# Order and pace of the weight loads between the two halves of a transformer layer

## The chip, the cores and the metric

The kernel runs on one core of one Trainium2 chip. The metric is the device time of one execution in microseconds (us); the program before the change took 205.26 us, the median of three runs (205.18, 205.26 and 205.62).

## What is computed

One layer on 2048 rows of width 448 in bf16: a linear attention with a learned feature map, then a gated feed-forward part, each behind a layernorm and with a residual. Cut to what matters:

```python
def _A_ref(x, wqkv, w_phi, wo):            # 16 heads of 28
    q, k, v = split_heads(x @ wqkv)
    pq, pk = q @ w_phi, k @ w_phi          # per head
    phi_q = concat([softmax(pq), softmax(-pq)]); phi_k = likewise of pk
    kv = einsum("bhsf,bhsd->bhfd", phi_k, v); z = phi_k.sum(s)
    o = (phi_q @ kv) / (phi_q @ z + 1e-6)
    return o @ wo
def _B_ref(x, w_gate, w_up, w_down):       # 448 -> 1792 -> 448
    return (sigmoid(x @ w_gate) * (x @ w_up)) @ w_down
h = x + _A_ref(layernorm(x), wqkv, w_phi, wo)
h2 = h + _B_ref(layernorm(h), w_gate, w_up, w_down)
```

## The kernel before, in words

The rows are cut into 16 tiles of 128. Three stretches follow one another. In the first, each tile is normed, transposed (xT4 to xT15 by DMA transposes that SP issues), multiplied by the folded key weights and by the value weights (pva, pvb), its features made (ek, ss, rs, phi) and its share added to the sum over all rows that the attention needs (the kv products kva0 to kva15 and kvb0 to kvb15, line 304 by way of `both`, in banks 6 and 7 of PSUM). In the transition, that sum is masked into kvz, the query features come from pqa and pqb with exponentials on ScalarE (eq, line 690), and per tile come num (the numerator and denominator), then on VectorE rsm, qq, b, c and rden (lines 767 to 775), the quotient o (line 779, on GpSimd or VectorE), its transpose oT (for tiles 0 and 1 on TensorE, line 506, for the others a DMA transpose that SP issues, line 792), the output projection woa and wob, a second layernorm and hT. In the third stretch, gate and up products ga and gb (line 304 by way of `pair`, line 876) alternate with the down products (dn, dp, later dm, line 908), each of which feeds an output store.

Nothing is planned at run time. The order of the instructions on each engine is written out by hand in `ORDER`, one list of names for each of SP, ScalarE (act), TensorE (pe), VectorE (dve) and GpSimd (pool). `Graph.op` records what each named operation reads and writes, and `Graph.emit` gives each one the semaphore waits that its dependencies (`deps`) call for; the engine works its list in order, so an instruction that waits holds all behind it on the same engine. SP's list holds all loads, transposes and stores. The weights of the transition and of the third stretch are 19 loads on SP's list (line 406), none of which waits for anything:

- ld_woe0, ld_woe1, ld_woo0, ld_woo1: the output projection, 336, 56, 336 and 56 KB, in rows of 896 bytes; first used by woa0 and wob0
- ld_wg0 to ld_wg3 and ld_wu0 to ld_wu3: gate and up, 448 KB each but 224 KB for ld_wg1 and ld_wu2, in rows of 3584 bytes. Every ga and gb depends on all eight of them (`wgu_keys`), so that ga0_1, the first, waits for the last to land
- ld_wd0 to ld_wd6: down, 224 KB each, in rows of 896 bytes; a down product over hidden columns ff needs ld_wd(ff // 2), and dn0_0 is the first

On SP's list before the change they stand behind the transpose xT15: sixteen of them in one row, in a mixed order, then oT2, then ld_wd0, ld_wu2 and ld_wd4, then oT3.

On TensorE's list the end of the first stretch reads "... pqa0_1 kvb12 pqb0_1 kva13 pqa1_0 kvb13 kva14 pqb1_0 kvb14 kva15 kvb15 qs pqa1_1 num0 pqb1_1 num1 pqa2_0 num2 pqb2_0 pqa2_1 oT0 oT1 pqb2_1 num3 woa0 wob0 num4 ... num6 ga0_1". One pq of the a kind is 8 matmuls, of the b kind 6; a kv product is 8, qs 32, a num 16. On VectorE's list: "kvzA kvzC kvzD rsm0 qq0 b0 c0 b1 rden0 c1 rsm2 rden1 qq2 b2 c2 rden2 o2 rsm3 qq3 b3 c3 rden3 bs2_0 ...". GpSimd makes o0, o1 and o3. num2 writes banks 6 and 7; pqa2_0 and pqb2_0 banks 0 and 1, pqa2_1 and pqb2_1 banks 4 and 5, which the exponentials eq1_1p and eq1_1m read before.

Of the kernel before, what the change touches and what calls it, by code (L numbers as in the profile page):

```python
# [18 lines left out]
class Graph:  # L19
# [86 lines left out]
    def emit(self, nc):  # L106
# [108 lines left out]
ORDER = {  # L215
# [6 lines left out]
    ),  # L222
# [60 lines left out]
    ),  # L283
}
PROGRAM = (
# [35 lines left out]
def build(nc, A_x, A_wqkv, A_w_phi, A_wo, B_w_gate, B_w_up, B_w_down, out):  # L321
# [10 lines left out]
    with ExitStack() as es:  # L332
# [66 lines left out]
        g = Graph()  # L399
# [163 lines left out]
        for kt in range(KT):  # L563
            b = (0, 1, 4, 5)[kt]
# [337 lines left out]
        def down1(t, b, parts, w=0):  # L902
            hb = hhT[(t // 4) % NHH]
            for nm, b, lo, hi in (("dm", b, 0, D - w), ("dl", 4, D - w, D))[:1 + (w > 0)]:
                for a, n in parts if nm == "dm" else ((0, 12), (12, 2)):
                    def f(e, a=a, n=n, b=b, lo=lo, hi=hi):
                        for ff in range(a, a + n):
                            p = e.matmul(bk(b)[:, lo:hi], lhsT=hb[:, ff, TS(t)], rhs=wd_sb[:, ff, lo:hi], start=ff == 0, stop=ff == FT - 1)  # L908
                        return p
                    op("pe", "%s%d_%d" % (nm, t, a), f,  # L910
                       r=[("hh", (t // 4) % NHH, ff, t % 4) for ff in range(a, a + n)] + [("wd", ff // 2) for ff in range(a, a + n)], w=[B(b)])
                finish(t, b, lo, hi, "" if nm == "dm" else "b")
# [9 lines left out]

        for step in PROGRAM.split():
            k, _, v = step.partition(":")
# [20 lines left out]
            elif k == "down1":  # L945
                down1(v[0], v[1], late, *v[2:])

        g.emit(nc)
        return g


def bass_sequential_preLN__linear_kernel_hedgehog__glu_gated_glu__prompt_kernel(
    nc, A_x, A_wqkv, A_w_phi, A_wo, B_x, B_w_gate, B_w_up, B_w_down, out
):
    build(nc, A_x, A_wqkv, A_w_phi, A_wo, B_w_gate, B_w_up, B_w_down, out)
# [28 lines left out]
```

## Time and profile before

| what | before |
|---|---|
| median of three runs | 205.26 us (205.18 to 205.62) |
| the profiled execution, its own time | 204.9 us |
| its span in the profile | 203.1 us |
| TensorE busy | 195.6 us, 96% of the span |
| VectorE, ScalarE, GpSimd busy | 134.7, 95.1 and 55.1 us |
| HBM read and written | 8.34 MB and 1.84 MB |

The profile is of one execution; times in it count from the start of the span, and what lies around the span (204.9 - 203.1 = 1.8 us) is not in it. PE is TensorE's matmuls, PEld its weight loads (one before each matmul), DVE is VectorE, ACT ScalarE, POOL GpSimd; SP only issues DMAs. A row of a timeline gives start, duration, engine, line, operation and tiles, and in square brackets how long the engine was idle before and what released it. The chain of waits is followed back from the last instruction and shown in order of time; "issue" in it is time in which the engine waited for nothing that the profile shows. A row of the windows view gives, for a stretch A:B, its length, then busy time and count of instructions of each engine, the granted clock, the mean busy share of the 16 DMA engines and what they moved in GB/s. A row of the DMA view gives a queue, its kind, packets, MB and share.

### The profile page before, as it was taken

The page shows a single profiled execution, that of the slowest core. Times are in us where ns is not written, and L with a number is a line of the kernel's source. Part 1 is how long each engine was busy: PE and PEld are TensorE (multiplying, and loading weights), DVE is VectorE, ACT ScalarE, POOL GpSimd, SP SyncE. Part 2 cuts the span into 40 slices and gives each one's busy share as a digit, 9 for nine tenths or more (in the row PEclk, how much of TensorE's full clock was granted, in tenths as well). Part 3 has the DMA queues.
Part 4 walks back from the last instruction along what each step waited for, and adds up shares of the span by engine and source line. Part 5 has one row for each costly group of instructions (what it writes and reads, how often), then busy time and mean ns, then how long its engine had stood idle before and what let it go on. Part 6 is the DMA issues. An engine that isn't in the chain of part 4 may idle for free.

```text
span 203.1 us, 5881 instructions
## 1 busy us (share of the span) xinstructions
PE 195.6 (96%) x2508; PEld 109.8 (54%) x2508; DVE 134.7 (66%) x328; ACT 95.1 (47%) x191; POOL 55.1 (27%) x97
## 2 busy tenths in 40 slices
PE   7899999997979999999999999999999999999995
PEld 2734555664448777777444544444555555554443
DVE  5899999977898897858667967526532422262224
ACT  3987989986982527222333343323422222222220
POOL 5698899613045303700023020001400000000000
PEclk9999999999999999999999999999999999999999
DMA  5966544999472411241004411030212000004003
GB/s 151 318 133 131 56 83 82 321 276 356 103 112 52 55 31 29 44 88 26 3 3 95 108 26 26 3 74 24 58 43 57 0 0 3 0 3 136 0 0 94
DMA packets 32867, 16.27 MB, mean 80 GB/s; under 512 B 25096, under 2 KB 31944, under 8 KB 32840
## 3 DMA queue, kind: packets, MB, share of 16 engines
q1 hardware_dynamic: 32336, 15.86, 32.9%
q8 instruction: 20, 0.33, 0.7%
q10 hardware_dynamic: 504, 0.03, 0.2%
q14 instruction: 7, 0.06, 0.1%
HBM read 8.34 MB, written 1.84 MB: 50 GB/s over the span
## 4 chain that ended last, share of the span: by engine, by line
PE 88%; DVE 6%; POOL 2%; issue 1%; DMA 1%; DVEq 0%
PE psum L304 81%; PE psum L908 5%; DVE st L513 2%; DMA x_sb<-in_A_x_dram 1%; DVE c_sb L773 1%; DVE b_sb L770 1%; POOL rst L526 1%; DVE st L798 1%; PE psum L581 0%; PE psum L506 0%; DVE mv L514 0%; POOL xn_pad L542 0%; DVE xnT L499 0%; POOL rst L816 0%; DVE rden L775 0%
## 5 line engine op out<-in xcount | busy, mean ns | idle before, releaser
L304 PE MATMUL psum<-xnT,wg_sb 64*128 64x512 bf16 (+1 forms) x490 | 93.1, 333 | 0.2 <-DVE rden L775 0.2
L304 PE MATMUL psum<-xnT,wu_sb 64*128 64x512 bf16 (+1 forms) x490 | 92.9, 333 | 0.0
L880 ACT ACTIVATE sg_sb<-psum 128x512 bf16<-128x512 f32 (+1 forms) x70 | 34.8, 511 | 91.5 <-PE psum L304 91.0
L881 DVE SCALAR_TENSOR_TENSOR hhT<-sg_sb,psum 128x512 bf16<-128x512 bf16 (+1 forms) x70 | 38.9, 576 | 53.2 <-ACT sg_sb L880 52.9
L304 PEld LDWEIGHTS psum<-xnT,wg_sb 64*128 64x128 bf16 x490 | 44.2, 94 | 23.3 <-DVE hhT L881 4.9
L304 PEld LDWEIGHTS psum<-xnT,wu_sb 64*128 64x128 bf16 x490 | 44.2, 94 | 13.4
L304 PE MATMUL psum<-wd_sb,hhT 64*128 64x448 bf16 x336 | 36.8, 349 | 0.0
L304 PEld LDWEIGHTS psum<-wd_sb,hhT 64*128 64x128 bf16 x336 | 17.0, 94 | 15.0 <-DVE x_sb L805 0.5
L304 PE MATMUL psum<-Wk,xnT 64*128 64x448 bf16 x112 | 22.0, 351 | 0.3 <-ACT Wk L499 0.2
L304 PE MATMUL psum<-wv_sb,xnT 64*128 64x448 bf16 x112 | 22.1, 351 | 0.1
L814 POOL TENSOR_SCALAR ve<-ssq 128x1 f32<-128x1 f32 x11 | 2.6, 234 | 57.8 <-ACT junk L811 57.5
L654 POOL TENSOR_TENSOR phi<-hhT,rs 128x896 bf16<-128x896 bf16 x10 | 16.9, 1701 | 2.5 <-DVE rs L650 1.6
L644 DVE TENSOR_REDUCE ss<-hhT 128x32 f32<-128x896 bf16 x16 | 16.9, 1063 | 0.5 <-ACT hhT L641 0.5
L690 ACT ACTIVATE eq<-psum 120x1024 bf16<-120x1024 f32 x16 | 15.7, 1026 | 2.7 <-PE psum L304 2.7
L304 PE MATMUL psum<-xnT,Wq 64*120 64x512 bf16 x112 | 14.7, 383 | 0.1
L304 PE MATMUL psum<-wo_o,oT 64*128 64x448 bf16 x56 | 13.2, 349 | 0.0
L304 PE MATMUL psum<-wo_e,oT 64*128 64x448 bf16 x56 | 13.1, 349 | 0.0
L915 DVE SCALAR_TENSOR_TENSOR x_sb<-psum,x_sb 128x448 bf16<-128x448 f32 (+2 forms) x17 | 9.4, 592 | 2.7 <-PE psum L908 1.6
L908 PE MATMUL psum<-wd_sb,hhT 128*128 128x448 bf16 (+2 forms) x70 | 11.1, 316 | 0.0
L304 PEld LDWEIGHTS psum<-Wk,xnT 64*128 64x128 bf16 x112 | 7.9, 94 | 5.9 <-PE psum L304 0.5
L779 POOL TENSOR_TENSOR o_pad<-c_sb,rden 128x448 bf16<-128x448 bf16 x8 | 7.4, 935 | 11.9 <-DVE rden L775 11.8
L770 DVE TENSOR_TENSOR b_sb<-psum,qq 128x464 bf16<-128x464 f32 x16 | 10.2, 638 | 0.3
(99 smaller groups left out, 236.4 us busy)
## 6 DMA issues: line engine op xcount, KB each, us to landing
out_dram<-x_sb SPq DMA_DIRECT2D x15, 112.0 KB, 1.8
x_sb<-in_A_x_dram SPq DMA_DIRECT2D x7, 224.0 KB, 4.5
wd_sb<-in_B_w_down_dram SPq DMA_DIRECT2D x7, 224.0 KB, 8.7
wg_sb<-in_B_w_gate_dram SPq DMA_DIRECT2D x3, 448.0 KB, 8.8
wu_sb<-in_B_w_up_dram SPq DMA_DIRECT2D x3, 448.0 KB, 7.9
wv_sb<-in_A_wqkv_dram SPq DMA_DIRECT2D x2, 224.0 KB, 4.7
wk_sb<-in_A_wqkv_dram SPq DMA_DIRECT2D x2, 196.0 KB, 3.8
wo_e<-in_A_wo_dram SPq DMA_DIRECT2D x1, 336.0 KB, 9.0
```

The lines of the kernel that those rows point to most:

```text
L304: p = e.matmul(o, lhsT=w, rhs=r, start=st, stop=sp, tile_position=(row, 0))
L513: op("dve", "bst%d" % t, lambda e: e.bn_stats(st1[:, t, :], x_sb[:, t, :]), r=[("x", t)], w=[("st1", t)])
L644: op("dve", "ss%d" % t, lambda e: e.tensor_reduce(ss[:, s, :].rearrange("p (b h) -> p b h", h=2), eks.rearrange("p b (d h) -> p b h d", h= ...
L654: return e.tensor_tensor(phi[:, sp, :, :, :].rearrange("p b a n -> p (b a) n")[:, :, 0:56].rearrange("p b (d h) -> p b d h", h=2), eks.rea ...
L690: op("act", "eq%d_%d%s" % (c, i, "pm"[sg]), lambda e, sg=sg: e.activation(eq[c][:, sg, 2 * i:2 * i + 2, :].rearrange("p g n -> p (g n)"), ...
L770: op("dve", "b%d" % t, lambda e: e.tensor_tensor(h3(b_sb), OMv[:, :, :, 0:EV], h2(qq)[:, :, :, None].to_broadcast([P, NB, 8, EV]), ALU.mul ...
L779: return e.tensor_tensor(o_pad[:, t % NO, off:off + D].rearrange("p (h d) -> p h d", h=H), c_sb[:, t % NS, :, 0:DH], rden[:, t % NS, :][:, ...
L814: op(("pool", "dve"), "ve%d" % t, lambda e: e.tensor_scalar(ve2[:, t:t + 1], ssq2[:, t:t + 1], 1.0 / D ** 3, EPS, op0=ALU.mult, op1=ALU.ad ...
L880: op("act", "sig" + nm, lambda e: e.activation(sg_sb[:, k, 0:N], bk(bg)[:, 0:N], ACT.Tanh, scale=0.5), r=[B(bg)], w=[("sg", k)])
L881: op("dve", "hh" + nm, lambda e: e.scalar_tensor_tensor(out=hhT[(t0 // 4) % NHH][:, ff, ns], in0=sg_sb[:, k, 0:N], scalar=1.0, in1=bk(bu)[ ...
L908: p = e.matmul(bk(b)[:, lo:hi], lhsT=hb[:, ff, TS(t)], rhs=wd_sb[:, ff, lo:hi], start=ff == 0, stop=ff == FT - 1)
L915: op("dve", "fin%d%s" % (t, nm), lambda e: e.scalar_tensor_tensor(out=h_sb[:, t, lo:hi], in0=bk(b)[:, lo:hi], scalar=0.5, in1=h_sb[:, t, l ...
```

## The change

Two things are changed on SP's list, and nothing on any other. The four loads of the output projection now come first, followed by gate and up in pairs, then down; and the load ld_wg1, the seventh of the row, is given a dependency on kva14, the last but one kv product of the a kind. SP therefore issues six loads behind xT15 (woe0, woe1, woo0, woo1, wg0, wu0), waits until kva14 is done, and then issues wg1, wu1, wg2, wu2, wg3, wu3, wd0, wd1 and wd2. The transposes oT2 and oT3 follow, and the last four loads of down, wd3 to wd6, stand between oT3 and oT4. The same 19 loads move the same bytes.

```diff
 ORDER = {
     "sp": (
...
-        "xT10 xT11 xT12 xT13 xT14 xT15 ld_wg0 ld_wu1 ld_wu3 ld_wd1 ld_wg1 ld_woe0 ld_wu0 ld_woe1 ld_woo0 ld_woo1 "
-        "ld_wg3 ld_wg2 ld_wd6 ld_wd2 ld_wd3 ld_wd5 oT2 ld_wd0 ld_wu2 ld_wd4 oT3 oT4 oT5 oT6 oT7 hT2 hT3 oT8 oT9 "
+        "xT10 xT11 xT12 xT13 xT14 xT15 ld_woe0 ld_woe1 ld_woo0 ld_woo1 ld_wg0 ld_wu0 ld_wg1 ld_wu1 ld_wg2 ld_wu2 "
+        "ld_wg3 ld_wu3 ld_wd0 ld_wd1 ld_wd2 oT2 oT3 ld_wd3 ld_wd4 ld_wd5 ld_wd6 oT4 oT5 oT6 oT7 hT2 hT3 oT8 oT9 "
...
 }
+PACE = {"ld_wg1": "kva14"}
...
+        at = {o.name: o.i for o in g.ops}
+        for a, b in PACE.items():
+            g.ops[at[a]].deps[at[b]] = False
         g.emit(nc)
```

## The prediction

> **What bounds the kernel now.** I read the page first, then the chain of waits, then the hole that the chain shows, by engine. On the page PE is busy for 96% of the span, and the GB/s row (40 slices of 5.1 us) has its tallest group in the eighth to tenth slice, where the weight loads run. The instruction queue q8 moved 20 packets.
>
> ```profile
> PE 195.6 (96%) x2508; PEld 109.8 (54%) x2508; DVE 134.7 (66%) x328; ACT 95.1 (47%) x191; POOL 55.1 (27%) x97
> ...
> GB/s 151 318 133 131 56 83 82 321 276 356 103 112 52 55 31 29 44 88 26 3 3 95 108 26 26 3 74 24 58 43 57 0 0 3 0 3 136 0 0 94
> ...
> q8 instruction: 20, 0.33, 0.7%
> ```
>
> The chain of waits, in order of time:
>
> ```profile
> 45.43 2.29 PE psum L304 x52
> 47.72 1.47 issue
> 49.19 1.86 PE psum L304 x24
> 51.04 0.55 PE psum L506 x8
> 51.60 1.04 PE psum L304 x22
> 52.63 0.02 issue
> 52.66 0.27 DVE rsm L767
> ...
> 60.82 0.04 issue
> 60.86 4.79 PE psum L304 x86
> 65.65 0.04 issue
> 65.69 60.42 PE psum L304 x858
> ```
>
> TensorE sets the end up to 52.63 and again from 60.86; between them it is mostly VectorE, step behind step. No weight load stands in the chain: the transition does not wait for its weights. What stands there is a hole of 1.47 us at 47.72, put down to "issue". The timeline of PE shows where it lies (the first row is for later):
>
> ```profile
> 42.44 0.39 PE L304 MATMUL psum<-v,phi 64*128 64x58 bf16 x16
> ...
> 47.46 0.25 PE L304 MATMUL psum<-kvz,eq 56*128 56x60 bf16 x6
> 49.19 0.32 PE L304 MATMUL psum<-kvz,eq 56*128 56x60 bf16 x10 [1.47 <-issue]
> ```
>
> Six and ten matmuls are the sixteen of num2. A semaphore is waited for ahead of a named operation, not inside it, so the hole is no wait of the program. I looked for missing instructions. The DMA view, asked for 29.9 to 30.0, 39.4 to 39.5, 46.6 to 46.7, 58.5 to 58.6, and for 58.5 to 129.2:
>
> ```profile
> q8 instruction: 1, 0.02, 61.6%
> ...
> q8 instruction: 1, 0.02, 55.4%
> ...
> q8 instruction: 1, 0.02, 72.9%
> ...
> q8 instruction: 1, 0.02, 93.8%
> ...
> q8 instruction: 8, 0.13, 0.9%
> ```
>
> And the windows view:
>
> ```profile
> 58.50:129.20 70.70, 69.39 (x1000) 43.00 (x1000) 54.14 (x153) 27.41 (x66) 14.96 (x27) 1.00 0.25 44
> ...
> 29.90:36.00 6.10, 6.10 (x134) 3.81 (x132) 6.00 (x11) 5.94 (x13) 5.75 (x5) 1.00 0.45 79
> ...
> 29.90:42.70 12.80, 12.80 (x268) 7.98 (x264) 12.36 (x22) 12.01 (x24) 9.33 (x7) 1.00 0.74 200
> 42.70:47.70 5.00, 4.91 (x132) 3.07 (x125) 3.78 (x9) 4.67 (x7) 0.00 (x0) 1.00 1.06 326
> ...
> 35.40:41.00 5.60, 5.60 (x120) 3.47 (x116) 5.30 (x10) 5.60 (x11) 4.04 (x3) 1.00 0.95 313
> 41.00:43.00 2.00, 2.00 (x42) 1.35 (x40) 1.97 (x4) 1.37 (x3) 0.14 (x1) 1.00 1.08 229
> 43.00:51.00 8.00, 6.43 (x147) 3.95 (x144) 5.79 (x16) 5.93 (x8) 1.87 (x2) 1.00 1.03 335
> ```
>
> Where DMA is quiet, 2000 PE and PEld instructions went through while 8 blocks came: one block for 250 of them (20 blocks for 2 x 2508 agrees). So q8 carries TensorE's code, and a block is asked for whenever TensorE has used one up. Counted on from the block of 29.9, the next was due after 266 instructions at about 36.0, and came at 39.4: 3.4 us late. The one after was due after some 530, at 42.7, and came at 46.6: 3.9 us late. From 42.7 to the hole TensorE used 257 more, one block, and was dry. The block took 72.9% of 0.1 us on 16 engines, 1.17 us, so to about 47.8; TensorE went on 1.4 us later, at 49.19. **The hole is code that came late because it was queued behind the weights**, and how late a block may be is the time that TensorE takes over the block before, less 1.2 + 1.4 = 2.6 us. I call the two blocks the fourth and the fifth. The fourth had 42.7 - 36.0 - 2.6 = 4.1 us and took 3.4; the fifth had 47.7 - 42.7 - 2.6 = 2.4 us and took 3.9, 1.5 too many.
>
> [...]
>
> **The change, part by part.** The issues of SP, before:
>
> ```profile
> 34.27 0.58 SPq L406 DMA_DIRECT2D wg_sb<-in_B_w_gate_dram  x1
> ...
> 41.92 3.34 SPq L406 DMA_DIRECT2D wd_sb<-in_B_w_down_dram  x4
> 52.33 1.21 SPq L792 DMA_TRANSPOSE oT<-o_pad  x1
> ...
> 57.39 1.20 SPq L792 DMA_TRANSPOSE oT<-o_pad  x1
> ```
>
> The first load is issued at 34.27; I take its data to flow from 35.4, 1.1 us on, where the stretch of 313 GB/s above begins (35.40 to 41.00).
>
> *First burst.* 784 KB of output projection and 896 KB of wg0 and wu0, 1.72 MB, from 35.4. At the 313 GB/s of 35.4 to 41.0 it is done at 40.9, at the 229 of 41 to 43 (small rows of wo and wd) at 42.9. The fourth block, due at 36.0, may come at 36.0 (nothing queued ahead) up to 42.9 (the whole burst ahead, at the slow rate); by the nearest row it is as late as before, 3.4 us, so 39.4. That is in time: it must start by 36.0 + 4.1 = 40.1. Cost taken: nothing.
>
> *The wait.* kva14 is the second half of the row at 42.44, done at 42.83. The wait costs SP nothing to speak of (it sat idle from 45.3 to 52.33), and TensorE a completion signal, between nothing and the 0.04 us of an "issue" row. Queued behind it are eight more weight loads and oT2, which is not ready before o2 anyhow. Data of the second burst flow from 42.9 + 1.1 = 44.0. The fifth block is due at 42.7 with the first burst drained, 1.3 us ahead of that data: it arrives at 42.7 + 1.2 + 1.4 = 45.3 and is needed at 47.7. **The hole goes.** Below nothing: the earliest end of the hole is no hole, so the gain has a top, 1.47.
>
> *What is late next.* VectorE, ScalarE and GpSimd around the hole:
>
> ```profile
> 48.03 0.60 DVE L773 TENSOR_TENSOR c_sb<-b_sb,psum 128x464 bf16<-128x464 bf16 x1
> 49.54 0.26 DVE L767 RECIPROCAL rsm<-psum 128x16 f32<-128x16 f32 x1 [0.92 <-PE psum L304]
> ...
> 51.67 0.62 DVE L779 TENSOR_TENSOR o_pad<-c_sb,rden 128x448 bf16<-128x448 bf16 x1
> 52.66 0.26 DVE L767 RECIPROCAL rsm<-psum 128x16 f32<-128x16 f32 x1 [0.36 <-PE psum L304]
> ...
> 46.55 1.94 ACT L690 ACTIVATE eq<-psum 120x1024 bf16<-120x1024 f32 x2 [0.29 <-PE psum L304]
> ...
> 48.19 0.93 POOL L779 TENSOR_TENSOR o_pad<-c_sb,rden 128x448 bf16<-128x448 bf16 x1 [7.05 <-DVE rden L775]
> ```
>
> num2 ends at about 47.9, but rsm2 waits for c1 (48.03 + 0.60 = 48.63): VectorE is 0.91 earlier from 49.54 on, not 1.47, and o2 ends at 52.29 - 0.91 = 51.38. On TensorE, pqa2_1 needs the exponential that ends at 46.55 + 1.94 = 48.49, so the two transposes can start at about 49.55; oT1 needs o1, which GpSimd can begin when o0 is done (49.12) and ends 0.93 later at 50.05. So oT1 ends at about 50.4 (before: 51.60) and num3 at 50.4 + 1.04 = 51.45 (before: 52.63). rsm3 starts at 51.5 instead of 52.66: 1.1 us earlier, between 0.91 (VectorE only) and 0.92 + 0.36 = 1.28 (all its idle time). From there the chain is unchanged work: ga0_1 at 59.75 instead of 60.86.
>
> *Second burst.* wg1 to wu3 are 2240 KB, 2.29 MB: at 335 GB/s landed at 50.9, at 229 at 54.0; ga0_1 at 59.75 doesn't wait. The sixth block, due at 47.7, comes by the 3.9 us of before at 51.6 and by the slow bound at 54.0, and is needed one block on, at about 58.5 - 1.1 = 57.4: in time. wd3 to wd6 follow oT3 (56.3), are issued from 57.5 in 4 x 0.6 us, ahead of oT4, which waits for o4 anyhow; 0.92 MB flow from 58.6 for 3 us. The first weight load of a down product is at 76.4:
>
> ```profile
> L304 PEld LDWEIGHTS psum<-wd_sb,hhT x336: 92/94/94, 76.4 to 180.0; 64*128 64x128 bf16 x168
> ```
>
> Cost taken: nothing; if oT4 did stand behind them, it would land up to 3 us later.
>
> **Sum:** -1.1 us, with nothing set against it. The profiled execution took 204.9, so 203.8 (span 202.0). The median of the runs shown lies 0.36 above it: 205.26 - 1.1 = 204.15, from 203.8 (-1.47) to 204.35 (-0.91).
>
> **The rivals.**
>
> *A small hole in another place.* The fourth block waits for nearly the whole first burst, 40.9 at 313 GB/s: 0.8 past its 40.1, a hole of up to 0.8 at 42.7 and none at 47.7. Against it: the delays of 3.4 and 3.9 us are, at 313 GB/s, of 1.1 to 1.2 MB, not of 1.7. For it: the small rows go first. Middle: 0.6 us lost of 1.1, 204.75.
>
> *The hole stays.* Either it isn't code at all, or the fifth block still falls behind weights: 250 instructions to a block is a mean, so 42.7 may be 43.4, and 44.0 is an estimate from one issue. Then it is late by 3.9 us as before and the time is 205.25. For it: 0.6 us is not much. Against it: a block's request before 44.0 has nothing ahead of it.
>
> [...]
>
> *Slower: one late block makes the next late.* If the fourth block comes at 41.9 (a first burst between 229 and 313 GB/s), TensorE goes dry at 42.7 until 41.9 + 2.6 = 44.5: 1.8 us, all on the path, since VectorE then waits for the last kv products. The fifth block is then asked for at 44.5, after the second burst's data began at 44.0, for kva14 was done before the hole. It is 3.9 late and makes the old hole of 1.1 again. 205.25 + 1.8 = 207.0; the point is a fourth block later than 41.4 (44.0 - 2.6), and there it costs 1.3, 206.55. I take a little past that point, 206.7. For it: at the slow rate the burst lasts to 42.9. Against: it takes the whole burst ahead of the block.
>
> **How the numbers follow.** Hole gone 0.62; small hole 0.10; hole stays 0.15; slower 0.13. About 0.2% (0.41 us: 204.85 to 205.67) is what a measurement of this kernel can tell from no change. Faster: 0.62 and most of the small hole, 0.70; same: the rest of that and the hole that stays, 0.17; slower 0.13. The range 203.7 to 205.4 takes in the first two and most of the third, some 0.85.
>
> **What would show it.** Right: no "issue" hole at 47.7; blocks of q8 near 39, 43 and 51; rsm3 near 51.5; ga0_1 near 59.75; span 202.0. Wrong: a hole near 42.7 (fourth block after 40.1), two holes, or one at 47.7 with the fifth block after 45; or ga0_1 released by a load.

## The result, and the profile after

The changed kernel takes 204.59 us (median of 20 runs, 204.21 to 206.07), the kernel before in the same comparison 205.28 (20 runs, 204.42 to 205.72). The ratio is 0.9971, 95% interval 0.9959 to 0.9984: 0.6 us less by the ratio (0.33 to 0.84), 0.69 by the medians. The profiled execution took 204.72 us with a span of 202.8. Line numbers are one higher than before, since the diff adds a line ahead of them.

The chain of waits of the changed kernel, in order of time, over the stretch where the hole was:

```profile
44.71 1.60 PE psum L305 x48
46.31 0.35 DVE rsm L740
...
48.29 0.55 DVE b_sb L771
48.84 0.17 DVE rden L776
49.01 0.07 issue
49.08 1.84 POOL o_pad L780 x2
50.91 0.05 issue
50.96 0.40 PE psum L507 x4
51.36 1.99 PE psum L305 x32
...
60.51 0.09 issue
60.59 4.79 PE psum L305 x86
65.38 0.04 issue
65.42 60.41 PE psum L305 x858
```

The piece "47.72 1.47 issue" is gone. In its place the chain runs from VectorE to GpSimd (o0, then o1) and to the transpose of o1: what was forecast as late next. Behind that transpose it stays on TensorE until 57.61, where before it went over to VectorE at rsm3; the two ways are level, since from rsm3 to ga0_1 it takes 8.17 us here (52.42 to 60.59) and took 8.20 before (52.66 to 60.86). From ga0_1 at 60.59 to the end of the span it takes 202.8 - 60.6 = 142.2 us, as before (203.1 - 60.86).

The timelines of VectorE, SP and PE in the changed kernel, on the same clock:

```profile
45.04 1.22 DVE L720 TENSOR_TENSOR kvz<-psum,mask 64x232 bf16<-64x232 f32 x3 [1.00 <-PE psum L305]
...
52.42 0.26 DVE L768 RECIPROCAL rsm<-psum 128x16 f32<-128x16 f32 x1 [0.24 <-PE psum L305]
```

```profile
35.24 1.19 SPq L407 DMA_DIRECT2D wo_e<-in_A_wo_dram  x2
...
38.26 2.26 SPq L407 DMA_DIRECT2D wu_sb<-in_B_w_up_dram  x1
43.76 0.47 SPq L407 DMA_DIRECT2D wg_sb<-in_B_w_gate_dram  x1
...
58.30 3.33 SPq L407 DMA_DIRECT2D wd_sb<-in_B_w_down_dram  x4
61.67 8.44 SPq L793 DMA_TRANSPOSE oT<-o_pad  x4
```

```profile
48.35 0.40 PE L305 MATMUL psum<-kvz,eq 56*128 56x60 bf16 x16
```

SP issued nothing from 40.52 to 43.76, though of its loads only wg1 has something to wait for. The sixteen matmuls of num2 now stand in one piece. But the whole transition lies later in this execution: the first kvz product starts at 45.04, against 44.15 in the profile of before (the row is quoted below with those of the other runs). The change touches nothing ahead of 34 us; 0.9 us were lost before that, where the two programs are the same. Counted from kvz, the transition up to ga0_1 takes 60.59 - 45.04 = 15.55 us, and took 60.86 - 44.15 = 16.71: 1.16 us less, of which this execution gave back 0.89 beforehand.

The DMA view of the changed kernel, for 37.9 to 38.1 and for 43.8 to 43.9, and the windows view of what TensorE did between its blocks of code (the fourth is the q8 line of 37.9 to 38.1, the fifth that of 43.8 to 43.9):

```profile
q8 instruction: 1, 0.02, 66.2%
...
q8 instruction: 1, 0.02, 70.1%
```

```profile
31.40:38.00 6.60, 6.60 (x131) 3.97 (x128) 6.46 (x13) 6.44 (x14) 6.37 (x5) 1.00 0.66 123
38.00:43.80 5.80, 5.80 (x126) 3.75 (x124) 5.65 (x10) 5.17 (x10) 2.61 (x2) 1.00 0.74 232
```

From the third block to the fourth 259 instructions, from the fourth to the fifth 250: both came when they were due, at one block for about 250. The data of the second burst, issued from 43.76, were not in front of the fifth: in the windows view the DMA engines move 0 GB/s from 44.00 to 44.90 and 155 from 44.90 on, 1.14 us after the issue.

### The profile page after: what moved, and what is told of

It reads as the page before. It is cut to its first block, busy times and chain, and to the rows that moved or that the text cites. A ratio compares the mean times of both kernels' runs of the same rounds, so it can differ in the third digit from the quotient of the medians.

```text
span 202.8 us, 5881 instructions
## 1 busy us (share of the span) xinstructions
PE 195.9 (97%) x2508; PEld 109.4 (54%) x2508; DVE 135.5 (67%) x328; ACT 95.7 (47%) x191; POOL 55.6 (27%) x97
## 4 chain that ended last, share of the span: by engine, by line
PE 84%; DVE 8%; POOL 2%; DMA 2%; issue 1%; SPq 1%; ACT 0%; DVEq 0%
PE psum L305 78%; PE psum L909 5%; DVE st L514 2%; DMA x_sb<-in_A_x_dram 2%; DVE ss L645 2%; POOL o_pad L780 1%; DVE b_sb L771 1%; DVE xn_pad L543 1%; SPq L407 1%; DVE c_sb L774 1%; PE psum L507 0%; POOL xn_pad L543 0%; DVE rs L651 0%; DVE xnT L500 0%; POOL rst L527 0%
```

## The experiments

The theory: TensorE ran dry because a block of its code was queued behind weights; the pause lets the block through. The main rival: the order of the loads, or num2 itself, or chance between executions, makes the difference. In the list names, kvz is the masked sum that VectorE makes at the start of the transition, and ga0_1 the first gate product at its end. Kernels compared together share their runs of the kernel before: b_again, a_again, a_nowait and b_wait; then b_shift, a_kva13, a_allwait and b_third.

**Both kernels again.** No edit.

> The kernel before, unchanged, for a second execution in the profile. Theory (late code): again the fifth block of TensorE's code starts 3 us or more after it is due, and TensorE stands still for 1.2 to 1.8 us inside or beside num2; from the start of the kvz products on VectorE to ga0_1 it takes 16.7 us as in the first profile; time within 0.2% of itself. Rival (what differs between the two profiles is chance): the hole is small or absent this time, and the two profiles of before differ in that stretch by 0.5 us or more. Either way the start of kvz (44.15 in the first profile) shows how far the first stretch, which the change doesn't touch, varies from one execution to the next.

> The changed kernel, unchanged, for a second execution in the profile. Theory (late code): no standstill of TensorE between the kv products and num3, kvz to ga0_1 in 15.5 us as in its first profile, 1.1 to 1.2 less than before; the ratio 0.997 as measured. If the first stretch alone took back part of the gain by chance, kvz starts nearer to 44.15 than to 45.04 this time and the span is about 202.0. Rival (the change makes the first stretch longer): kvz starts at 45.0 again, and the ratio stays at 0.997 because of it.

> The kernel before, unchanged, a third execution in the profile. Theory: a hole again after 1474 instructions, of 0.8 to 2 us, and kvz to ga0_1 takes 15.15 us plus the hole (15.5 without one), as in the first two (1.57 and 16.71; 0.87 and 16.03). Rival: no relation between the two.

Measured, from the profiles and the comparisons:

| kernel | hole in the chain, us | kvz starts, us | kvz to ga0_1, us | ratio to before, 95% |
|---|---|---|---|---|
| before (first profile) | 1.47 | 44.15 | 16.71 | |
| b_again | 0.77 | 44.02 | 16.03 | 0.9981 (0.9960 to 1.0002) |
| b_third | 0.97 | 44.83 | 16.20 | 0.9988 (0.9968 to 1.0007) |
| changed (first profile) | none | 45.04 | 15.55 | 0.9971 (0.9959 to 0.9984) |
| a_again | none | 44.08 | 15.52 | 0.9945 (0.9924 to 0.9966) |
| a_nowait | 2.72 | 44.92 | 17.96 | 1.0030 (1.0004 to 1.0057) |
| b_wait | none | 44.76 | 15.51 | 0.9939 (0.9916 to 0.9961) |
| a_kva13 | none | 44.68 | 15.51 | 0.9943 (0.9923 to 0.9964) |

The timeline of b_again: kvz, num2 with its hole, ga0_1.

```profile
44.02 1.22 DVE L719 TENSOR_TENSOR kvz<-psum,mask 64x232 bf16<-64x232 f32 x3 [0.99 <-PE psum L304]
...
47.33 0.25 PE L304 MATMUL psum<-kvz,eq 56*128 56x60 bf16 x6
48.36 0.32 PE L304 MATMUL psum<-kvz,eq 56*128 56x60 bf16 x10 [0.77 <-issue]
...
60.05 0.27 PE L304 MATMUL psum<-xnT,wg_sb 64*128 64x256 bf16 x1 [0.22 <-DVE rden L775]
```

The fifth block of b_again, in its DMA view for 45.8 to 45.9:

```profile
q8 instruction: 1, 0.02, 69.6%
```

69.6% of 0.1 us on 16 engines are 1.11 us, so it was in at about 46.9, and TensorE went on 1.4 us later, as in the first profile.

The kernel before, with its row for kvz of the first profile:

```profile
44.15 1.22 DVE L719 TENSOR_TENSOR kvz<-psum,mask 64x232 bf16<-64x232 f32 x3 [0.99 <-PE psum L304]
```

The hole is there in all three executions of before, behind the same six matmuls of num2, but 0.77, 0.97 and 1.47 long. The 0.77 of b_again is a miss of the theory, which gave 1.2 to 1.8, and the two profiles of before differ in the transition by 0.68 us, as the rival had it: the length of the hole is to a good part chance, its place is not. (The expectation of b_third gives the same two holes as 1.57 and 0.87, 0.1 longer than the chain of waits has them; hence its 15.15.) In the four profiles with the hole in num2, the transition takes the hole plus 15.23 to 15.26 us; without a hole it takes 15.51 to 15.55. So about 0.28 us of any hole there costs nothing, and the rest is paid in full. And kvz starts at 44.0 to 45.0 in either kernel (44.08 in a_again, 45.04 in the first profile of the changed one): the late start is the spread of the first stretch, not the change. The ratio of a_again is better than the 0.997 expected: the same kernel gains 0.6 us in the first comparison and 1.1 in this one, and the kernel before itself came out 0.4 us under its other runs (0.9981).

**The order without the wait, and the wait without the order.** The first edit, a_nowait, is to the changed kernel; the second, b_wait, to the kernel before, which keeps its own order of loads.

```diff
-PACE = {"ld_wg1": "kva14"}
+PACE = {}
```

```diff
+PACE = {"ld_wu0": "kva14"}
...
+        for a, b in PACE.items():
+            g.ops[at[a]].deps[at[b]] = False
```

> The changed order of the loads without the wait for kva14. Theory (late code): with fifteen loads issued in one row the fifth block falls behind weights again; it starts 3 us or more after it is due, TensorE stands still for 1 to 2 us at the end of the kv products or in num2, and the ratio to before is 0.999 to 1.003. Rival (the order of the loads brings the gain, not the pause): no standstill, ratio 0.997.

> The order of before, with only the wait added: ld_wu0, the seventh load, waits for kva14. Theory (late code): the first burst of 1.95 MB is drained by about 42, the fifth block starts when it is due and the hole goes as in the changed kernel; kvz to ga0_1 in 15.5 us, ratio 0.996 to 0.998. If 1.95 MB is too much, the fourth block starts after 40.1 and a small hole stands near 42.7. Rival (the order brings the gain): hole as before, ratio 1.000.

The timeline of a_nowait:

```profile
44.92 1.22 DVE L720 TENSOR_TENSOR kvz<-psum,mask 64x232 bf16<-64x232 f32 x3 [1.00 <-PE psum L305]
...
48.24 0.25 PE L305 MATMUL psum<-kvz,eq 56*128 56x60 bf16 x6
51.21 0.32 PE L305 MATMUL psum<-kvz,eq 56*128 56x60 bf16 x10 [2.72 <-issue]
...
62.88 0.27 PE L305 MATMUL psum<-xnT,wg_sb 64*128 64x256 bf16 x1 [0.20 <-DVE rden L776]
```

and of b_wait:

```profile
44.76 1.22 DVE L720 TENSOR_TENSOR kvz<-psum,mask 64x232 bf16<-64x232 f32 x3 [1.00 <-PE psum L305]
...
48.07 0.40 PE L305 MATMUL psum<-kvz,eq 56*128 56x60 bf16 x16
...
60.27 0.27 PE L305 MATMUL psum<-xnT,wg_sb 64*128 64x256 bf16 x1 [0.20 <-DVE rden L776]
```

The new order alone has the longest hole of all, longer than the 1 to 2 us expected, at the same six matmuls, and is slower than before (1.0030, interval above 1). The wait alone removes the hole and gives all of the gain, with the old mixed order; its 0.9939 is again better than expected (0.996 to 0.998). Its fourth block came at 39.9 to 40.0 by the DMA view, just ahead of the 40.1 that the prediction gave it, and no hole follows at 42.7. The DMA view of a_nowait for 48.4 to 48.6 has the fifth block, and its windows view the instructions ahead of it:

```profile
q8 instruction: 1, 0.02, 38.4%
```

```profile
31.50:43.50 12.00, 12.00 (x246) 7.45 (x244) 11.71 (x21) 11.21 (x23) 8.76 (x6) 1.00 0.76 207
43.50:48.50 5.00, 4.90 (x130) 3.05 (x123) 3.77 (x9) 4.67 (x7) 0.00 (x0) 1.00 0.99 280
```

The third block came at 31.5; 490 instructions, two blocks of about 250, had gone by 43.5, and 253 more when the fifth came at 48.5: some 5 us late, while the DMA engines were 99% busy. The pause is what the change lives on; the order of the loads is not.

**The count of instructions, shifted.** The warm-up matmuls at the start are cut smaller, so that 64 more TensorE instructions stand ahead of everything else.

```diff
-        for i, (n, size) in enumerate(((9, 512), (1, 128), (1, 128), (2, 128), (1, 128), (8, 128), (4, 128), (7, 128), (9, 128), (2, 128))):
+        for i, (n, size) in enumerate(((41, 80), (1, 128), (1, 128), (2, 128), (1, 128), (8, 128), (4, 128), (7, 128), (9, 128), (2, 128))):
```

> The kernel before with the nine warm-up matmuls of 512 columns at the very start replaced by forty-one of 80 columns: 64 more instructions of TensorE at about the same time, nothing else. In three profiles with a hole it began after the same number of TensorE instructions, 1474 counted from the start. Theory (late code): the hole follows the count, not the operation: again after 1470 to 1478 instructions, which is now 32 matmuls earlier in the program, in the last matmuls of pqb1_1 instead of the seventh of num2; it lasts 0.8 to 3 us, and the time is 204.5 to 206.5. Rival (num2 itself, its banks or what runs beside it, makes the hole): it stays at the seventh matmul of num2, after 1538 instructions.

The timeline of PE in b_shift:

```profile
45.97 0.40 PE L304 MATMUL psum<-kvz,eq 56*128 56x60 bf16 x16
46.21 0.62 PE L304 MATMUL psum<-xnT,Wq 64*120 64x512 bf16 x4
47.54 0.43 PE L304 MATMUL psum<-xnT,Wq 64*120 64x512 bf16 x2 [0.71 <-issue]
47.75 0.41 PE L304 MATMUL psum<-kvz,eq 56*128 56x60 bf16 x15
```

The hole has left num2 and stands inside pqb1_1, behind its fourth matmul of six, ahead of num1: 32 matmuls earlier in the program. The windows view counts what TensorE had done when it began, first in the kernel before, then in b_shift:

```profile
0.00:47.72 47.72, 45.44 (x724) 26.05 (x725) 42.69 (x98) 40.51 (x81) 32.83 (x55) 1.00 0.73 180
```

```profile
0.00:47.50 47.50, 43.53 (x724) 26.52 (x725) 42.89 (x97) 39.70 (x79) 33.42 (x55) 1.00 0.72 177
```

724 matmuls and 725 weight loads in both, and in the holes of b_again, b_third and a_nowait too. With the 24 waits and the like that the view leaves out, 1473 instructions stand ahead of the hole, and the 1474th of the expectation is the first behind it. The hole follows the count of instructions, so it is code that is missing, and num2, its banks and its operands have nothing to do with it. The blocks agree: the fifth starts at 46.6, 45.8, 46.9, 48.5 and 44.8 (before, b_again, b_third, a_nowait, b_shift; DMA views), and TensorE goes on at 49.19, 48.36, 49.37, 51.21 and 47.54, each time 2.5 to 2.7 us later. The prediction had 1.2 + 1.4 = 2.6. The hole, 0.71, is a little shorter than the 0.8 to 3 us expected. Here all of it is paid: kvz at 44.69 to ga0_1 at 60.91 is 16.22, less 0.71 is 15.51, what it takes without a hole. The ratio is 1.0034 (1.0007 to 1.0061), and the hole alone does not make it: in this profile it is no longer than before, but the stretch from ga0_1 to the end takes 142.8 us in place of 142.2, and the difference arises just ahead of 97.0, where TensorE waits 0.36 us for a transpose xnT. Why that came late is open. The new warm-up itself is shorter (it ends at 4.30, in the profile of before at 5.27).

**How much room the wait has.** The wait moved to the kv product before, about 0.9 us earlier.

```diff
-PACE = {"ld_wg1": "kva14"}
+PACE = {"ld_wg1": "kva13"}
```

> The changed kernel with the wait for kva13 in place of kva14, about 0.9 us earlier: data of the second burst flow from about 43 instead of 44, and the fifth block is due at 42.7 to 43.5. Theory (late code, what counts is what is queued when the block is due): it is on the edge; if the block starts within 0.7 us of 1237 instructions there is no hole and the ratio is 0.994 to 0.998; if it falls behind data it starts 2 us or more late and the hole is 0.5 to 2 us. Rival (any pause between the bursts is enough): no hole, block on time.

wg1 was issued at 42.28 (SP's timeline), and the DMA view for 43.2 to 43.3 has the fifth block:

```profile
42.28 0.47 SPq L407 DMA_DIRECT2D wg_sb<-in_B_w_gate_dram  x1
```

```profile
q8 instruction: 1, 0.02, 78.1%
```

On time by the count of the trace (after 1232 instructions, waits included; 1237 in the changed kernel's first profile and 1224 in a_again), no hole, ratio 0.9943. By the 1.1 us from issue to data that the prediction used, the block was in by 0.1 to 0.2 us. The rival's reading (any pause will do) isn't excluded by this run; a still earlier wait wasn't tried.

**Everything behind the wait.**

```diff
-PACE = {"ld_wg1": "kva14"}
+PACE = {"ld_woe0": "kva14"}
```

> The changed order with all of the loads behind the wait: ld_woe0, the first, waits for kva14. 4.70 MB then flow in one burst from 44 to about 58. Theory (late code): fourth and fifth block come on time, no hole in num2; the sixth is due at 47.7 with the whole burst ahead or coming: if a block waits for all that was queued before it, it starts between 51 and 54 and there is no hole; if it waits for all of the burst, it starts near 58, past the 54.8 that it may, and a hole of up to 3 us stands between num4 and ga0_1. ga0_1 waits for gate and up, landed at about 56 to 57.5, hardly if at all. Time 204.3 without a new hole, up to 207 with one. Rival (the weights must be early): ga0_1 or woa0 is released by a load, 1 us or more late.

208.88 us, ratio 1.0164 (1.0131 to 1.0197). There is no hole in num2, and kvz to ga0_1 takes 15.51. The sixth block came at 50.6, with the burst still being issued (until 53.0): near the 51 to 54 of a block that waits for what was queued before it, far from the 58 of one that waits for the whole burst. The loss comes behind, in the chain of waits and on PE:

```profile
56.59 0.53 DVE c_sb L774
57.12 7.43 DMA oT<-o_pad
64.55 0.05 issue
```

```profile
64.60 0.55 PE L305 MATMUL psum<-wo_e,oT 64*128 64x448 bf16 x1 [2.28 <-DMA oT<-o_pad]
```

```profile
61.00:64.60 3.60, 1.32 (x25) 1.03 (x21) 1.98 (x4) 0.71 (x2) 1.35 (x2) 0.97 1.35 138
64.60:66.00 1.40, 1.40 (x8) 0.57 (x10) 0.00 (x0) 0.00 (x0) 0.00 (x0) 0.50 1.10 378
66.00:68.00 2.00, 2.00 (x36) 1.52 (x34) 1.10 (x4) 0.00 (x0) 0.83 (x1) 0.56 0.83 211
```

Neither reading named it. The rival had woa late, but by a load; it is woa2, held by the transpose oT3, which is issued by SP behind 4.7 MB of weights and takes 7.43 us to land. From ga0_1 to the end it takes 207.0 - 60.6 = 146.4 us, 4.2 more than the 142.2 of the others (142.8 in b_shift). 2.3 of them are the wait. After it the granted clock was 0.50 for 1.4 us and 0.56 for 2; the matmuls of woa2 took 0.55 to 0.58 us, one pair 0.35 to 0.37 us after the other, against 0.35 and 0.17 to 0.19 in the changed kernel. By an estimate from the clock (half of 1.4 and 0.44 of 2) that is about 1.6 of the other 1.9. This is the price of a wait set on too much: the transposes behind it.

No kernel tried is faster than the changed one by more than the intervals; b_wait, a_again and a_kva13 (0.9939 to 0.9945) can't be told apart.

## Why the prediction was right, and how far its size holds

The forecast was 204.15 us, 1.1 less than before; measured were 0.69 less, on the side and in the range that were forecast. The mechanism is the one that was forecast; the size is less sure.

- **Late code.** Shown: the hole moves with the count of instructions (b_shift), grows to 2.72 us when the loads come in one row (a_nowait), and goes with the pause, whatever the order of the loads (b_wait). The rival "the hole stays" is out. TensorE was dry after one block without supply in five profiles: 257 instructions after the fifth block was due in the first, 253 in a_nowait, and behind 724 matmuls and 725 weight loads in each. Not shown is what exactly a late block waits behind. The trace has the start of its packet, not when it was asked for; in a_nowait some 1.4 MB of weights moved between the two by the count of instructions (5 us at 280 GB/s). So how the DMA engines share their time between code and weights stays open; "queued behind the weights" is the author's reading of blocks that came 3.4 to 5 us late beside a burst.
- **The first burst.** The fourth block was taken to be as late as before, 3.4 us. It came on time at 38.0, after 259 instructions. That was harmless, and neither the small hole at 42.7 nor the slower cascade came.
- **The wait.** Data from 44.0 were forecast and the fifth block ahead of them at 42.7; wg1 was issued at 43.76 and the block came at 43.8, in an execution that ran 0.9 late. The sixth block, due near 48.5 (252 instructions after the fifth), came at 51.5 behind the second burst, 3 us late, close to the 51.6 forecast, and TensorE did not miss it. The pause does not do away with lateness; it moves it to a block for which there is time.
- **What is late next.** rsm3 was forecast at 51.5 and ga0_1 at 59.75; with the 0.89 us of the late start these are 52.4 and 60.64, and the profile has 52.42 and 60.59. The cushion of VectorE, c1 and o1 was rightly placed: 1.16 us gained of a hole of 1.47 (0.31 kept; 0.28 in the table).
- **The second burst, wd3 to wd6 behind oT3.** No load stands in the chain, and 142.2 us from ga0_1 to the end are unchanged. The four loads were issued from 58.30 and kept SP until 61.63, so that oT4 went out at 61.67, at once behind them; it was no loss, but with less room than the prediction said.
- **The size** is the weak term. The hole of 1.47 us was read off one execution and taken for the kernel's. Three executions of before have 1.47, 0.77 and 0.97, a mean of 1.07; less the 0.28 that is free, 0.8 is to be had, which agrees with the 0.69 measured (0.33 to 0.84). But the later comparisons of kernels without the hole gave more, 1.13 us (a_again), 1.17 (a_kva13) and 1.25 (b_wait), with intervals from 0.7 or 0.8 to 1.6 or 1.7, while the kernel before came out 0.4 and 0.25 us under its own other runs (b_again, b_third). So the comparisons put the gain between 0.6 and 1.25 us. That the 1.1 of the forecast was too much is likely by the three holes, and not shown by the times.

## What to carry to other kernels

Where an engine is idle inside one operation and no semaphore explains it, count its instructions. A hole that comes after the same count in every execution (724 matmuls and 725 weight loads in five profiles), one block of code (here about 250) after a block was due, and beside a burst of loads, was here code that came late beside data; moving the count (by 64 in b_shift) is a cheap way to test it. A pause in the loads at the moment when the next block is due was enough (the shortest tried left SP without an issue from 40.1 to 42.3, in a_kva13), but nothing urgent may stand behind it on the same queue (in a_allwait oT3 took 7.43 us to land, and TensorE waited 2.28). And take the size of such a stall from several executions: here it ran from 0.77 to 1.47 us in three of one kernel.

## What the runs showed of the hardware that was not expected

- A hole of 2.72 us in a_nowait left the granted clock at 1.00 (the windows view gives 1.00 for 51.2 to 56), a wait of 2.28 us in a_allwait, 2.3 us after another of 1.06 (which ended at 60.01), was followed by 0.50 for 1.4 us and 0.56 for 2. Which difference decides was not tried.
- DMA transposes that SP issued behind weights landed late: 11.0 us for oT2 and 7.43 for oT3 in a_allwait, where the median of the transposes of oT is 2.5.
- The first stretch, the same code in all of these kernels but for the warm-up of b_shift, ended between 44.0 and 45.1 us in ten profiles. That is as much as the change is worth, and it is why one profile of each kernel can't size it.
